# One list scheduler places every step of a scan, a router and eight experts

## The chip, the cores and the metric

The kernel runs on one core of a Trainium2 chip. Its time is the device time in microseconds (us) of one launch; the kernel before took 975.37 us, the median of three runs (975.14 to 976.99). Five engines work side by side, each through its own list of instructions in a fixed order: TensorE (PE in the rows), VectorE (DVE), ScalarE (ACT), GpSimd (POOL) and SyncE (SP), which here only issues transfers. They wait for each other by semaphores.

## The reference, cut to what matters

```python
sig = 1.0 / (1.0 + np.exp(-f_logit))
f = lower_bound + (1.0 - lower_bound) * sig          # x, f_logit: (4, 5056, 256)
for t in range(S):
    h = f[:, t] * h + (1.0 - f[:, t]) * x[:, t]
    y[:, t] = h
x = y.reshape(N, 256)                                 # N = 20224 tokens
logits = x @ w_gate                                   # 8 experts
e_idx = argmax(logits); gate_w = softmax(logits)[e_idx]
eom = 1.0 / (1.0 + np.exp(-(x @ w_output_gate)))
for e in range(8):
    m = e_idx == e
    out[m] = gate_w[m] * eom[m, e] * (np.maximum(x[m] @ w1[e], 0) @ w2[e])   # 256 -> 1024 -> 256
```

## The kernel before, in words

Tokens lie along the free axis and channels on the partitions. There are 40 chunks of 512 tokens, called c0 to c39 here; each goes through the same steps: loads (L257, L258), a tanh (L278), products (L282), the forget gates (L287), the scan (L293), a sum of squares (L300, L304) that sets a power of two as scale (L149 to L157, five short VectorE steps), the scaled values split in a high and a low fp16 part (L325 on ScalarE, L329 on VectorE), four DMA transposes that turn channels into rows (L320), the gate matmuls (L344), a short router on VectorE and ScalarE (L363 to L462) that ends with the row number of each token in its expert's list (`dst`, L448), and four row scatters on GpSimd (L467) into a scratch in DRAM, sorted by expert.

Each expert's two weight matrices, in two halves each, are loaded (L595), a Gram matmul gives a bound of their norm (L607, L614, L621), a power of two follows from it, and ScalarE and VectorE split them into high (L643) and low fp16 parts (L648). A product of two fp16 pairs is three matmuls.

Tiles of tokens of one expert are gathered from the scratch by a DMA transpose (`xq`, L660) that SyncE issues after it has read the tile's address. There are 16 early tiles of 128 tokens, two per expert in two rounds: the first round needs the rows of three chunks, the second of five. In an early tile each half of the up projection is 24 matmuls (L765 to L767), then a relu (L769, `eh`), its low part (L776, `el`), and each half of the down projection 12 matmuls (L785 to L787). 64 tiles of 256 follow (L712 to L714 up, L752 to L754 down), then smaller ones; their experts are chosen by a plan on VectorE, made whenever four more tiles are sure. The result is scaled (L679, L798) and scattered to the output (L802).

What sets the order: the first part, up to the first tile of 256, is written by loops over weight halves that pump a few stages of the chunks at a time, and a scheduler of the framework then moves instructions on some engines within it; from there on `experts` gives each quarter of a tile its share of the work by hand, in that order.

## Time and profile before

| what | value |
|---|---|
| median of three runs | 975.37 us |
| profiled execution, and its span in the trace | 981.98 us, 980.2 us |
| TensorE busy | 905.3 us (92% of the span) |
| VectorE, ScalarE, GpSimd busy | 796.2, 514.0, 382.1 us |
| mean granted clock of TensorE | 0.992 of 2.4 GHz |

Shares are means over stretches with different limits, so the rows further down are read by stretch. A line such as L712 is a line of the kernel before. A duration in a row is that of one instruction; neighbours on an engine overlap, so a distance between two starts is often shorter.

### The profile page before, as it was taken

The numbers are of one execution on the slowest core, as the hardware profiler recorded it, in microseconds if no ns is written. First come the engines' busy times: TensorE is split into PE (matmuls) and PEld (weight loads), VectorE is DVE, ScalarE is ACT, GpSimd is POOL, SyncE is SP. The second block draws the span as 40 slices with busy tenths as digits, with TensorE's granted clock in tenths as the row PEclk, the third lists the DMA queues.
The fourth block names the chain that finished last, engine by engine and source line by source line (L and its number), as shares of the span: only waits on it lengthen the run. The fifth ranks groups of instructions, "written<-read, shape, count | busy, mean of one in ns | idle before, by whom it ended". The sixth has DMA issues, their size and how long they took to land.

```text
span 980.2 us, 30989 instructions
## 1 busy us (share of the span) xinstructions
PE 905.3 (92%) x9775; PEld 813.9 (83%) x9775; DVE 796.2 (81%) x2683; ACT 514.0 (52%) x1075; POOL 382.1 (39%) x380
## 2 busy tenths in 40 slices
PE   2258878899999999999999999999999999999997
PEld 2247868788888888888888888888888888899986
DVE  7989877799898889888988889888898877846653
ACT  5667666555555555555555555555555543323332
POOL 1423324345444445543444454444444533312112
PEclk9999989999999999999999999999999999999999
DMA  8899973866555667565655555676665543412211
GB/s 312 208 286 290 247 211 95 184 149 146 151 157 155 153 140 153 143 148 145 167 153 149 138 154 139 147 165 155 145 154 138 151 118 84 118 44 50 50 35 34
DMA packets 236528, 146.16 MB, mean 149 GB/s; under 512 B 200508, under 2 KB 202173, under 8 KB 236369
## 3 DMA queue, kind: packets, MB, share of 16 engines
q1 hardware_dynamic: 220784, 101.34, 43.6%
q0 software_dynamic: 15296, 42.73, 14.5%
q8 instruction: 93, 1.52, 0.6%
q14 instruction: 67, 0.54, 0.2%
q10 hardware_dynamic: 288, 0.02, 0.0%
HBM read 58.38 MB, written 44.23 MB: 105 GB/s over the span
## 4 chain that ended last, share of the span: by engine, by line
PE 70%; issue 11%; DMA 9%; DVE 4%; POOL 3%; ACT 1%; SPq 1%; another core or an unknown queue 0%; POOLq 0%; DVEq 0%; ACTq 0%
PE ph L712 11%; PE py L752 11%; PE ph L714 11%; PE ph L713 10%; PE py L754 10%; PE py L753 10%; DMA xq<-scr 4%; DMA out_dram<-yo,mt 3%; POOL out_dram L802 2%; PE ph L765 1%; PE ph L767 1%; PE ph L766 1%; DMA w<-in_wT_dram 1%; PE pr L344 1%; PE pg L607 1%
## 5 line engine op out<-in xcount | busy, mean ns | idle before, releaser
L712 PE MATMUL ph<-xq,w 128*128 128x256 f16 (+2 forms) x1312 | 326.0, 259 | 1.0 <-DMA xq<-scr 1.0
L714 PE MATMUL ph<-xq,w 128*128 128x256 f16 (+2 forms) x1312 | 326.5, 259 | 0.2 <-issue 0.2
L713 PE MATMUL ph<-xq,w 128*128 128x256 f16 (+2 forms) x1312 | 326.3, 259 | 0.0
L717 ACT ACTIVATE hh<-ph 128x512 f16<-128x512 f32 (+1 forms) x312 | 173.4, 556 | 283.4 <-PE ph L714 246.3
L752 PE MATMUL py<-w2s,hh 128*128 x1136 | 309.0, 272 | 1.3 <-issue 0.7
L754 PE MATMUL py<-w2s,hl 128*128 x1136 | 309.4, 272 | 0.1
L753 PE MATMUL py<-w2s,hh 128*128 x1136 | 309.2, 272 | 0.0
L802 POOL DMA_INDIRECT out_dram<-yo,mt x146 | 153.6, 1052 | 308.7 <-ACT yo L798 255.5
L467 POOL DMA_INDIRECT scr<-rows,dst x154 | 191.9, 1246 | 182.9 <-issue 110.1
L725 DVE SCALAR_TENSOR_TENSOR hl<-ph,hh 128x512 f16<-128x512 f32 (+1 forms) x312 | 198.2, 635 | 44.5 <-ACT hh L717 28.3
L687 DVE COPY w<-w1s 128x2048 f16 x164 | 114.9, 701 | 44.7 <-PE ph L714 39.1
L712 PEld LDWEIGHTS <-w 128*128 128x128 f16 x1312 | 127.6, 97 | 12.7 <-DVE w L687 1.3
L714 PEld LDWEIGHTS <-w 128*128 128x128 f16 x1312 | 127.4, 97 | 11.9
L713 PEld LDWEIGHTS <-w 128*128 128x128 f16 x1312 | 127.3, 97 | 10.0 <-issue 0.3
L754 PEld LDWEIGHTS <-hl 128*128 128x128 f16 x1136 | 110.7, 97 | 13.8 <-issue 0.4
L752 PEld LDWEIGHTS <-hh 128*128 128x128 f16 x1136 | 110.8, 98 | 12.7 <-ACT hh L717 1.0
L753 PEld LDWEIGHTS <-hh 128*128 128x128 f16 x1136 | 110.7, 97 | 10.6
L293 DVE TENSOR_TENSOR_SCAN xt<-ft,xt 128x512 f32<-128x512 f32 (+4 forms) x78 | 90.8, 1172 | 0.0
L798 ACT ACTIVATE yo<-py,fac 128x256 f32<-128x256 f32 (+1 forms) x146 | 61.7, 467 | 26.9 <-PE py L754 25.7
L329 DVE SCALAR_TENSOR_TENSOR ft<-xt,sa,ft 128x512 f16<-128x512 f32 (+1 forms) x76 | 55.8, 739 | 20.6 <-ACT ft L278 19.9
L325 ACT ACTIVATE ft<-xt,sa 128x512 f16<-128x512 f32 (+1 forms) x76 | 50.2, 707 | 38.1 <-DVE li L312 29.1
L344 PEld LDWEIGHTS <-ft 128*128 128x128 f16 x600 | 51.3, 98 | 14.7 <-ACT ft L325 4.9
(189 smaller groups left out, 1353.4 us busy)
## 6 DMA issues: line engine op xcount, KB each, us to landing
ft<-in_fT_dram SPq DMA_DIRECT2D x37, 512.0 KB
xt<-in_xT_dram SPq DMA_DIRECT2D x37, 512.0 KB
w<-in_wT_dram SPq DMA_DIRECT2D x32, 512.0 KB
scr<-rows,dst POOLq DMA_INDIRECT x154
rows<-ft SPq DMA_TRANSPOSE x152
out_dram<-yo,mt POOLq DMA_INDIRECT x146
xq<-scr SPq DMA_TRANSPOSE x98
scr<-padt SPq DMA_DIRECT2D x9, 136.0 KB
```

The lines of the kernel that those rows point to most:

```text
L293: nc.vector.tensor_tensor_scan(out=xt[:, k, a:z], data0=ft[:, k, a:z], data1=xt[:, k, a:z], initial=init, op0=ALU.mult, op1=ALU.add)
L467: ins = nc.gpsimd.indirect_dma_start(out=scr[:, :], out_offset=IOA(ap=dst[:, b : b + 1], axis=0), in_=rows[:, b, :], in_offset=None)
L687: nc.vector.tensor_copy(out=w, in_=w1f[:, ds(T["ev"] * (2 * WH) + h * 2 * QH, 2 * QH)])
L712: nc.tensor.matmul(out=o, lhsT=w[:, f, k, 0, :], rhs=T["xh"][:, k, 0:n], start=first, stop=False)
L713: nc.tensor.matmul(out=o, lhsT=w[:, f, k, 0, :], rhs=T["xl"][:, k, 0:n], start=False, stop=False)
L714: nc.tensor.matmul(out=o, lhsT=w[:, f, k, 1, :], rhs=T["xh"][:, k, 0:n], start=False, stop=last)
L717: nc.scalar.activation(hh[:, :, 0:n], ph[:, :, 0:n], AF.Relu)
L725: nc.vector.scalar_tensor_tensor(out=hl[:, :, 0:n], in0=ph[:, :, 0:n], scalar=0.0, in1=hh[:, :, 0:n], op0=ALU.max, op1=ALU.subtract)
L752: nc.tensor.matmul(out=o, lhsT=hh[:, i, c], rhs=wh, start=first, stop=False, skip_group_check=True)
L753: nc.tensor.matmul(out=o, lhsT=hh[:, i, c], rhs=wl, start=False, stop=False, skip_group_check=True)
L754: nc.tensor.matmul(out=o, lhsT=hl[:, i, c], rhs=wh, start=False, stop=last, skip_group_check=True)
L802: ins = nc.gpsimd.indirect_dma_start(out=out[:, :], out_offset=IOA(ap=T["mt"][0 : T["p"], b, 2:4].bitcast(I32), axis=0), in_=T["yo"][0 : T ...
```

## The change

The loops and the pumping are gone. Every step is now an `Op` with an engine, a cost, the steps that it needs and a rank; `Clock.drive` simulates all engines at build time, takes at each point, among the steps that can start first, the one with the lowest rank, and emits the program in that order, which is then fixed on every engine. Ranks stand in a table by kind of step and chunk (shown in the diff by two lines).

With it come edits of the work itself. The first three chunks (FLIP) are turned into rows by 16 TensorE transposes each, and two ScalarE copies (`settle`), in place of four DMA transposes. Raw weights are loaded into the place of the next expert's fp16 weights, and all sixteen first loads follow each other. The norms of weights come in four groups (TEAMS), so that the five short scale steps run 4 times and not 16. For the first ten chunks (QUICK) eight more gate matmuls per chunk replace a ScalarE and a VectorE step. Small steps move from VectorE to ScalarE: the scales `sa` and `li`, the sum with 1 (`more_eg`), and the factors of early tiles. The early tiles follow a table of rounds and experts (ORDER). Where chunk 10 and later scatter rows, scatters stand at least 2.7 us apart in the simulated time (GAP), and all but a chunk's first are held behind the VectorE instruction that came last before them. A gather waits for those scatters only that no earlier gather has waited for.

```diff
+RANK = {
+    "setup": (-296.2,),
+    "pad": (-360.65,),
+    "steady": (147.22, -373.75, -143.82, 119.77, -79.5, -359.56, -45.81, 165.38,),
+    "tiles": (160.19, -324.31, -321.43, -288.45, -270.77, 131.32, -298.94,),
+    "first": (46.53,),
...
+FLIP = 3
+QUICK = 10
+NEAR = 0.2
+ORDER = ((0, 1), (0, 0), (0, 2), (1, 3), (1, 0), (0, 3), (1, 2), (0, 6), (0, 5), (1, 1), (1, 7), (0, 4), (1, 5), (1, 6), (0, 7), (1, 4))
+SHORT = 0.25
+TEAMS = ((0,), (1, 2), (3, 4), (5, 6, 7))
+GAP = 2.7
...
+    def start(self, o):
...
+        if o.gap:
+            t = max(t, self.sent + GAP)
...
+    def drive(self, lines, stop):
+        while not stop():
+            best = {}
+            lines = [line for line in lines if not line.over()]
+            for line in lines:
+                for o in line.heads():
+                    t = self.start(o)
+                    if t is not None:
+                        best.setdefault(o.eng, []).append((t, RANK[o.group[0]][o.group[1]] + o.shift, o))
+            assert best
+            pick = []
+            for e, c in best.items():
+                first = min(x[0] for x in c)
+                near = [x for x in c if x[0] <= first + NEAR]
+                p = min(near, key=lambda x: (x[1], x[0]))
+                fill = [x for x in near if x[2].cost <= SHORT and x[0] + 0.06 < p[0]]
+                pick.append(min(fill, key=lambda x: (x[1], x[0])) if fill else p)
+            t, _, o = min(pick, key=lambda x: x[0])
+            self.run(o, t)
+            for line in lines:
+                q = line.queues.get(o.eng)
+                if q and q[0] is o:
+                    q.pop(0)
...
-        nc.vector.tensor_scalar(sa, na, sx, None, ALU.mult)
-        nc.vector.tensor_tensor(out=li, in0=ix, in1=gi4, op=ALU.mult)
...
+            nc.scalar.activation(H["sa"], na, AF.Copy, scale=H["sx"])
...
+            nc.scalar.activation(H["li"], gi4, AF.Copy, scale=H["ix"])
...
+        def flip(i):
+            if i == 0:
+                H["rt"] = [pp.tile([P, 2, 2 * D], F16, tag="h", name="rt", bufs=4) for _ in range(nb // 2)]
+            for b in range(nb):
+                for k in range(KD):
+                    q = i * KD + k
+                    nc.tensor.transpose(
+                        out=H["rt"][b // 2][:, b % 2, q * P : (q + 1) * P], in_=hl[:, i, k, b * P : (b + 1) * P],
+                        identity=ident,
+                    )
+
+        def settle(j):
+            nc.scalar.activation(rows[:, 2 * j : 2 * j + 2, 0:CM].bitcast(F16), H["rt"][j], AF.Copy)
...
+                if i == 0 and quick:
+                    o, g = pr[:, b, 0:G], wgs[:, k, 1, :]
+                    nc.tensor.matmul(
+                        out=o, lhsT=hl[:, 0, k, tok], rhs=g, start=(k == 0), stop=False, skip_group_check=True
+                    )
...
+        def more_eg():
+            nc.scalar.activation(H["eg"][:, 0:nb], H["eg"][:, 0:nb], AF.Copy, bias=1.0)
...
+        if c < FLIP:
+            op(8, TEN, 0.5, lambda: flip(0), ["h0", "h1"], "flip", ring=("h", 4, (c, "settle1")), lazy=True)
+        turn1 = []
+        op(10, TEN, 0.45, all_gates, ["l0", "l1", ("setup", 11)], "pr", lag=2.8)
+        if c < FLIP:
+            op(10, TEN, 0.5, lambda: flip(1), ["l0", "l1"], ("turned", c), ring=("h", 4, (c, "settle1")), lazy=True)
+            for j in range(nb // 2):
+                op(10, ACT, 1.05, lambda j=j: settle(j), [("turned", c), *gone], f"settle{j}", lazy=True)
...
+            op(16, GPS, 1.32, lambda b=b: send(b), ["dst", "noted", "iota", *([f"settle{b // 2}"] if c < FLIP else ["turn00", "turn01", "turn10", ("turned", c)])],
+               "sent" if b == nb - 1 else None, ship=0.7, late=AHEAD <= c < NCH - 1 and b > 0, gap=AHEAD <= c < NCH - 1)
...
+    def crude(e, h, z):
+        if e == E - 1:
+            r = spare[:, h * WH : (h + 1) * WH]
+        else:
+            r = (w1f, w2f)[h][:, (e + 1) * 2 * WH : (e + 2) * 2 * WH].bitcast(F32)
+        return r[:, z * QH : (z + 1) * QH]
...
+        new = [k for k in new if id(k) not in waited]
...
-    ordered(0, prog["cut"])
+    ordered(0, 0)
```

SyncE, from where the last first loads of weights stand. Before, `ft` and `xt` are buffers of chunks, `w1s` and `w2s` places that c0 and c3 borrow:

```order
L595 DMA w_167<-in_wT_dram 128x1024
L595 DMA w_169<-in_wT_dram 128x1024
L320 DMA_TRANSPOSE w1s_126<-w2s_127 128x4x128 x4
L257 DMA w1s_126<-in_fT_dram 128x2x512
L258 DMA w1s_126<-in_xT_dram 128x2x512
L320 DMA_TRANSPOSE rows1_133<-ft_147 128x4x128 x4
L320 DMA_TRANSPOSE rows0_132<-ft_155 128x4x128 x4
L257 DMA ft_465<-in_fT_dram 128x2x512
L258 DMA xt_466<-in_xT_dram 128x2x512
L320 DMA_TRANSPOSE rows1_133<-w1s_126 128x4x128 x4
```

```order
L893 DMA w2s_119<-in_wT_dram 128x1024 x2
L893 DMA w1s_118<-in_wT_dram 128x1024 x2
L893 DMA w2s_119<-in_wT_dram 128x1024 x2
L445 DMA fx1_127<-in_fT_dram 128x2x512
L445 DMA fx1_127<-in_xT_dram 128x2x512
L445 DMA fx3_129<-in_fT_dram 128x2x512
L445 DMA fx3_129<-in_xT_dram 128x2x512
L893 DMA w1s_118<-in_wT_dram 128x1024
L893 DMA spare_125<-in_wT_dram 128x1024 x4
L893 DMA w1s_118<-in_wT_dram 128x1024
L893 DMA w2s_119<-in_wT_dram 128x1024
L994 TENSOR_LOAD pf_tab_705
```

Four transposes for each of c0, c1, c2 stood between the loads, and the next chunks' loads behind them; after, the loads of c3 and c4 (`fx1`, `fx3`) follow the weights and no transpose stands before the first gather's address is read.

ScalarE, around the first hi parts of weights (L643 before, L955 after). L363 are logit copies before; L525 and L529 are scales, L558 the copies of transposed rows after:

```order
L363 ACTIVATE lgp_283<-pr_258,li_227 128x128
L300 ACTIVATE ft_155,hss_212<-xt_156 128x512 x2
L417 ACTIVATE ex_357<-dl_306 128x32
L643 ACTIVATE w1s_126<-w_151,ws_299 128x8x128
L643 ACTIVATE w1s_126<-w_153,ws_299 128x8x128
L363 ACTIVATE lgp_362<-pr_330,li_256 128x128
L419 ACTIVATE eg_359<-gs_327 128x4
L325 ACTIVATE ft_155<-xt_156,sa_320 128x512 x2
L278 ACTIVATE w1s_126<-w1s_126 128x512 x2
L417 ACTIVATE ex_434<-dl_379 128x32
L363 ACTIVATE lgp_439<-pr_407,li_325 128x128
L287 ACTIVATE w1s_126<-w1s_126,fb_100,fa_99 128x512 x2
```

```order
L514 ACTIVATE fx0_126,hss_247<-fx0_126 128x512 x2
L529 ACTIVATE li_317<-gi4_113,xi_229 128x2
L955 ACTIVATE w1s_118<-w1s_118,ws_288 128x8x128
L529 ACTIVATE li_327<-gi4_113,xi_296 128x2
L955 ACTIVATE w1s_118<-w1s_118,ws_288 128x8x128
L525 ACTIVATE sa_339<-na_104,xs_295 128x2
L532 ACTIVATE fx3_129<-fx3_129,sa_339 128x512
L558 ACTIVATE spare_125<-rt_273 128x2x512
L558 ACTIVATE spare_125<-rt_274 128x2x512
L532 ACTIVATE fx3_129<-fx3_129,sa_339 128x512
L955 ACTIVATE w2s_119<-w2s_119,ws_288 128x4x256
L641 ACTIVATE ex_424<-dl_416,li_317 128x32
```

The first copies out of PSUM stand between the high parts (L532) of another chunk, with two more hi parts of weights behind them, and the logit copies are gone.

GpSimd, from the first scatter of rows (L467 before, L706 after) on; L802 and L1179 write an early tile's result:

```order
L467 DMA scr_72<-w1s_126,dst_381 162944x544 x4
L467 DMA scr_72<-rows1_133,dst_478 162944x544 x4
L467 DMA scr_72<-rows0_132,dst_537 162944x544 x4
L421 IOTA rows1_133 128x4
L421 IOTA rows0_132 128x4
L467 DMA scr_72<-rows1_133,dst_736 162944x544 x4
L421 IOTA rows1_133 128x4
L802 DMA out_0_dram<-ey_1001,mt_669 20224x256
L467 DMA scr_72<-rows0_132,dst_1141 162944x544 x4
L802 DMA out_0_dram<-ey_1244,mt_893 20224x256
```

```order
L706 DMA scr_75<-spare_125,dst_533 162944x544 x4
L706 DMA scr_75<-rows1_124,dst_568 162944x544 x2
L651 IOTA rows0_123 128x4
L706 DMA scr_75<-rows1_124,dst_568 162944x544 x2
L706 DMA scr_75<-rows0_123,dst_693 162944x544 x4
L1179 DMA out_0_dram<-ey_1074,mt_786 20224x256
L1179 DMA out_0_dram<-ey_1213,mt_830 20224x256
L651 IOTA rows0_123 128x4
L651 IOTA rows1_124 128x4
L706 DMA scr_75<-rows0_123,dst_1370 162944x544 x3
L706 DMA scr_75<-rows1_124,dst_1362 162944x544 x4
L651 IOTA rows1_124 128x4
```

c0 to c2 are scattered in one row in both. Before, c3's and c4's scatters stand one chunk at a time with a tile's result between them and the next; after, two results come first, and then c4's and c3's scatters nearly together.

## Rows read from the trace of the kernel before

**Rows 1.** Busy time by stretches: us, PE, PEld, DVE, ACT, POOL, granted clock, DMA, GB/s.

```profile
0.00:60.00 60.00, 14.48 (x179) 11.45 (x180) 49.59 (x191) 37.29 (x73) 15.80 (x35) 1.00 0.90 262
60.00:105.00 45.00, 36.78 (x504) 34.06 (x504) 41.08 (x139) 31.78 (x53) 15.10 (x14) 0.96 1.07 300
105.00:196.00 91.00, 78.52 (x1026) 70.77 (x1023) 69.37 (x241) 54.99 (x102) 32.59 (x32) 0.94 0.75 173
196.00:800.00 604.00, 603.35 (x6017) 540.67 (x6018) 529.50 (x1774) 328.73 (x700) 272.06 (x252) 1.00 0.60 149
```

**Rows 2.** The chain of waits, 40 to 200 us: start us, us, what.

```profile
43.79 2.08 ACT w2s L643 x2
...
54.80 5.81 DMA xq<-scr
...
80.05 4.77 DMA scr<-rows,dst
...
111.24 0.41 PE pr L344 x16
...
191.17 5.11 DMA xq<-scr
...
196.41 0.27 PE ph L712
```

**Rows 3.** The timeline of TensorE, 140 to 147 us: start us, us, engine, line.

```profile
143.29 0.22 PE L765 MATMUL ph<-xq,w1s 128*128 128x128 f16 x1
...
144.63 0.27 PE L785 MATMUL py<-w2s,eh 128*128 128x256 f16 x1
...
145.94 0.17 PE L621 MATMUL pb<-l,ones 128*128 128x1 bf16 x1
```

**Rows 4.** Groups by line and form, ScalarE, 0 to 188.8 us: busy us, mean ns.

```profile
L769 ACT ACTIVATE eh<-ph 128x512 f16<-128x512 f32 x32 | 18.8, 588 | 18.6 <-PE ph L767 9.4 <-remote 5.4 <-PE pb L621 2.6
L643 ACT ACTIVATE w1s<-w,ws 128x1024 f16<-128x1024 f32 x16 | 17.4, 1138 | 2.0 <-DVE ws L155 2.0
...
L798 ACT ACTIVATE ey<-py,fac 128x256 f32<-128x256 f32 x15 | 7.0, 465 | 10.4 <-PE py L787 5.0 <-remote 3.5 <-PE pr L344 1.9
L363 ACT ACTIVATE lgp<-pr,li 128x128 f32<-128x128 f32 x10 | 3.6, 362 | 12.6 <-remote 5.8 <-PE pr L344 5.0 <-PE ph L767 1.9
...
L417 ACT ACTIVATE ex<-dl 128x32 f32<-128x32 f32 x9 | 2.0, 221 | 1.7 <-DVE dl L383 1.0 <-issue 0.7
```

**Rows 5.** Groups of VectorE, 0 to 188.8 us, and its timeline at 75 us.

```profile
L329 DVE SCALAR_TENSOR_TENSOR ft<-xt,sa,ft 128x512 f16<-128x512 f32 x16 | 11.6, 742 | 0.0
...
L679 DVE TENSOR_SCALAR fac<-mt,cinv 128x1 f32<-128x1 f32 x16 | 3.3, 205 | 2.1 <-DMA mt<-scr 1.0 <-issue 1.0
...
L309 DVE TENSOR_SCALAR sa<-na,xs 128x2 f32<-128x2 f32 x10 | 2.5, 248 | 0.0
L149 DVE TENSOR_SCALAR wv<-pb 128x1 f32<-128x1 f32 x16 | 2.4, 148 | 0.3 <-PE pv L304 0.3
...
L368 DVE TENSOR_TENSOR lgo<-lgp 128x64 f32<-128x64 f32 x10 | 2.2, 216 | 5.1 <-ACT lgp L363 5.1
...
75.00 0.18 DVE L448 TENSOR_REDUCE dst<-pos 128x4 int32<-128x32 f32 x1
```

**Rows 6.** The timeline of GpSimd, 30 to 54 and 190 to 205 us.

```profile
33.96 1.46 POOL L467 DMA_INDIRECT scr<-w1s,dst  x1 [30.56 <-DVE w1s L282]
...
47.86 0.96 POOL L467 DMA_INDIRECT scr<-rows,dst  x1 [0.30 <-issue]
49.12 0.96 POOL L467 DMA_INDIRECT scr<-rows,dst  x1 [0.30 <-issue]
...
52.54 0.14 POOL L421 IOTA rows<- 128x4 int32 x1 [2.29 <-DMA scr<-rows,dst]
...
194.79 1.41 POOL L467 DMA_INDIRECT scr<-rows,dst  x1 [2.83 <-issue]
...
200.87 1.42 POOL L467 DMA_INDIRECT scr<-rows,dst  x1 [0.30 <-issue]
```

More of the change, by code (lines that the diff above doesn't have):

```diff
@@ L344, in gates @@
                 nc.tensor.matmul(
-                    out=o, lhsT=hl[:, i, k, tok], rhs=g, start=(i == 0 and k == 0), stop=(i == 1 and k == KD - 1),
+                    out=o, lhsT=hl[:, i, k, tok], rhs=g, start=(i == 0 and k == 0 and not quick), stop=(i == 1 and k == KD - 1),
                     skip_group_check=True,
                 )
-        for b in range(nb):
-            for i in range(2):
-                aside(gates, i, b)
-        when = LATER if between["on"] else (10, 10)
-        def turns(stage):
-            for k in range(KD):
-                if when[k] == stage:
-                    pace(turn(1, k))
@@ new lines, in chunk @@
+        for k in range(KD):
+            op(4, ACT, 0.75, lambda k=k: square(k), [f"scan{k}"] + ([(c - 2, "pv")] if c >= 2 else []), f"sq{k}")
+        op(5, TEN, 0.08, bound, ["sq0", "sq1", ("setup", 1), *past], "pv")
+        steps = pow2(H, lambda: pv, TX, "x", ("sx", "ix"))
+        chain(6, VEC, 0.19, steps[0], ["pv"])
+        for i, fn in enumerate(steps[1:4]):
+            chain(6, VEC, 0.18, fn, (), "sx" if i == 2 else None)
+        chain(6, VEC, 0.18, steps[4], (), "ix", lazy=True)
+        last.pop(VEC)
@@ new lines, in chunk @@
+        if not quick:
+            op(11, ACT, 0.34, logits, ["pr", "li"], "lgp")
+            chain(12, VEC, 0.22, sum_logits, ["lgp"], "lgo")
+        last[VEC] = "pr" if quick else "lgo"
+        for fn in (peak, below, keys, first_key, hot, own, gate):
+            chain(12, VEC, 0.21, fn, (), {below: "dl", hot: "oh", gate: "gs"}.get(fn))
+        if c >= AHEAD:
+            for x in turn1:
+                op(*x, ship=0.9, late=True)
+        op(14, TEN, 0.16, all_before, ["oh"], "pk", lag=1.4)
@@ L807, in put @@
             apart(ins, "out")
[L810 to L811 removed]
+    prog = {"places": ""}
     total = sure(N)
     unsure = (N - 256 * total - WHOLE * (P // 2 + 1) + E * (P - 1)) // P
[L814 to L829 removed]
@@ L977, in tile_scan_moe @@
-    while turns[-1] < E or line or pend or mid or over:
-        mine, rest = early(nh)
-        step(DRAIN, mine, LEAD)
-        rest()
-        if slots and prog["got"] == 0:
-            ahead(0)
-    prog["cut"] = len(nc.cur_bb.bb.instructions)
-    wp.release()
-    mpool["m"] = ctx.enter_context(tc.tile_pool(name="mp", bufs=2))
+    end = total + WHOLE + HALF
+    late = 2
+    last_put = end - late - REST
+    padded, known, tiles = {}, {}, {}
+    clock = Clock()
+    clock.tail = lambda: nc.cur_bb.bb.instructions[-1].name
@@ new lines, in tile_scan_moe, with spread, fn @@
+    clock.hold = lambda ins, name: tc.add_manual_dep(raw(ins), name, DATA, reason="pace")
+    clock.flush = beside
+    def spread(gen, count, needs, key, group, shift=0.0):
+        at = {}
+        def fn(i):
+            if i == 0:
+                at["g"] = gen()
+                next(at["g"])
+            kind = next(at["g"], None)
+            assert bool(kind) == (i < count - 1)
+        return [
+            Op(VEC, 0.2, lambda i=i: fn(i), needs if i == 0 else [(*key, i - 1)], key if i == count - 1 else (*key, i),
+               group=group, shift=shift)
+            for i in range(count)
+        ]
@@ new lines, in pad_op @@
+    def pad_op():
+        scattered["pad"] = [pad()]
+    lines = [Line(setup())]
+    for e in range(E):
+        lines.append(Line(expert_load(e)))
+        lines.append(Line(weights(e)))
+    chunks = []
+    for c in range(NCH):
+        lines.append(Line(chunk_load(c)))
+        chunks.append(chunk(c))
+        lines.append(Line([o for o in chunks[c] if not o.lazy and o.group[0] != "s"]))
+        lines.append(Line([o for o in chunks[c] if o.lazy]))
+    lines.append(Line([o for ops in chunks for o in ops if o.group[0] == "s"]))
@@ L987, in ordered @@
+    for t in range(end + 1):
+        for q in range(4):
+            work["pe"] += ([up(t, q)] if t < end else []) + ([down(t - 1, q)] if t else [])
+    lines += [Line(ops) for ops in work.values()]
+    clock.drive(lines, lambda: all(o.done for ops in work.values() for o in ops))
+    for line in lines:
+        assert line.over()
+    beside()
+    prog["got"] = end
     def ordered(start, cut):
@@ L995, in ordered, with experts @@
             prev[ins.engine] = ins.name
[L997 to L1000 removed]
+    def experts(t0, t1):
         for t in range(t0, t1 + 2):
+            if t < t1:
+                fetch(t)
             T = tiles.get(t) if t < t1 else None
```

1105 lines of the change are left out of this document (619 added, 486 removed), and 7 rows, old and new, of the table RANK.

## The prediction

> **What bounds the kernel now.** I read the busy time by stretches first, then the chain of waits, then single engines around the places that the chain names. The stretches [rows 1] say where anything can be won. From 196 to 800 us TensorE is busy 603.35 of 604 us at full clock. Before 196 us it is busy 14.48 + 36.78 + 78.52 = 129.8 of 196 us, so 66.2 us are idle there, and the granted clock of 105 to 196 us is 0.94. The diff keeps every matmul of the tiles, so a gain can come only out of these 196 us; after them an order can only lose.
>
> The chain of waits [rows 2] gives the events of the start. The gather of the first early tile is issued at 54.80 and takes 5.81 us, so TensorE begins early tiles at 60.6. The gathers of later tiles are what it waits for: behind the scatters of the fifth chunk (c4; chunks count from c0) rows land for 4.77 us from 80.05 to 84.8. The first tile of 256 has run alone when the gather of the next lands at 196.3 (191.17 + 5.11) and L712 starts at 196.41 for good. That lone first tile has 48 matmuls of L712 to L714 at 0.109 us (the spacing of the 256-column matmuls below), 5.2 us of work that is done, so before's steady stage behaves as one that began, without a gap, at 196.4 - 5.2 = 191.2. This is the mark that after has to beat.
>
> **The change part by part.**
>
> First chunks. The 12 DMA transposes of c0 to c2 leave SP; 48 transposes on TensorE and six copies on ScalarE take their place. TensorE is nearly empty there (14.48 of 60 us [rows 1]), so I take the spacing of its 128-column matmuls, 0.056 us ((144.63 - 143.29) / 24 [rows 3]): 48 x 0.056 = 2.7 us, beside other waits and at no cost. The upper bound is one matmul's whole duration each, 0.22: 10.6 us. A word of the Trainium skill on this, in two sentences that nothing else needs. "TensorE: Matmul & The Clock Gate", Part 4, gives about 275 ns for one 128x128 transpose inside a kernel, says that it needs a copy out of PSUM, and that such transposes don't hold the clock up; by it the 48 would be an estimated 13.2 us, and this speaks against the edit. No run here has such a transpose yet; the nearest row is the 0.22 us above.
>
> The copies (128x1024 f16 out of PSUM) have no row of their own either. The nearest are a ScalarE copy of that size out of SBUF, 1.138 us, and a relu of half the size out of PSUM, 0.588, twice 1.18 [rows 4]. I take 1.138, and as neighbours on ScalarE overlap by 0.10 (two copies of 1.138 in 2.08 us in the chain [rows 2]), 1.04 each.
>
> Where this lands: ScalarE stands in one queue from 7.5 us on, and the order shows what is before the place on which the fifth chunk rests (its L419 before, L646 after): 65 activations before, 88 after. By kind and with the overlap taken off: 6 copies x 1.04 = 6.2; 2 more hi parts of weights x 1.04 = 2.1; 4 more relus x 0.49 = 2.0 (three early tiles now stand ahead, one before); 2 evacuations x 0.365 = 0.7; 16 small ones that VectorE did (scales, +1, factors), 0.22 by L417 [rows 4], 0.12 with the overlap, = 1.9; minus 5 logit copies x 0.26 = 1.3. Sum 11.6 us. This is the term that costs. Its low end is 0, if the idle time of ScalarE hides it (31.78 of 45 us busy from 60 to 105 us [rows 1]).
>
> VectorE. Removed up to the first steady tile: 12 chains of five steps, 60 x 0.148 = 8.9; ten each of L309 and L368, 2.5 + 2.2, and the 16 factors, 3.3 [rows 5]; with three smaller kinds at 0.15 to 0.19 (23 of them, 3.9) some 21 us of durations. Up to c4's dst alone I get +2.0 us, as four more el and the rest of the Gram norms now come earlier and the short steps of a chunk follow each other directly, each waiting for the one before. VectorE is therefore not the later of the two engines at that place, ScalarE is.
>
> The fourth tile (T4). Before, c4's dst starts at 75.00 [rows 5]. After: 75.00 + 11.6 = 86.6. Both c3 and c4 are then scattered together: 8 scatters 1.26 apart (47.86 to 49.12 [rows 6]) are 10.1, so 96.7; the last lands 2.5 us after its end (50.08 to 52.54 [rows 6]; 4.77 at the worst [rows 2]), 99.2; and the gather takes 5.81 [rows 2]: 105.0. The three tiles ahead of T4 need no such time: their x comes some 3 us later than before, at 63.5 (the first scatter waits for some 6 us more of copies and small steps on ScalarE, about 40 instead of 33.96 [rows 6], and behind it the queue of twelve is the same, less the slow spacing of before's first ones), and three tiles are 3 x 2 x (1.34 + 1.31) = 15.9 us, over by 80. They fill idle time of TensorE; what T4 starts is then without a wait:
>
> From T4 to the first steady matmul. Half an up projection is 144.63 - 143.29 = 1.34 us, half a down 145.94 - 144.63 = 1.31 [rows 3]. Left are 26 x 1.34 + 28 x 1.31 = 71.5 us, and gates and counts of five chunks, about 0.8 each, 4.0 (24 gate matmuls at 0.026, by the 16 in 0.41 us of the chain [rows 2], are 0.6): 75.5. The clock costs too: 0.94 on average from 105 to 196 us [rows 1], between full speed and the lower level, is some 5.5 us, in a stretch that has idle times; with fewer of them I take 3.0. First steady matmul 105.0 + 75.5 + 3.0 = 183.5. By their orders and the rows' means VectorE and ScalarE have 64 and 61 us of work in these 78 us and don't bound it, and by the same count the dst of the eighth chunk, the last that the first steady tiles need, comes near 138.
>
> Steady stage. Scatters are held at least 2.7 us apart: four take 8.1 us instead of 200.87 - 194.79 = 6.1 [rows 6]. Price 0 as long as a plan's rows are waited for by a gather that TensorE reaches later; at worst 2 us for each plan of four tiles, 16 of them, 32 us. I take 0, as TensorE has no idle there now [rows 1]. The moves from VectorE to ScalarE in it are 0 as well: neither bounds.
>
> Sum. 183.5 - 191.2 = -7.7 us on the profiled execution of 981.98 (span 980.2 and 1.8 around it): 974.3. It stands 6.6 us above the median of the runs, 975.37, so 967.7 there.
>
> **The rivals.**
>
> More is won. ScalarE's 20 us of idle before c4 take up the 11.6, and only VectorE's +2.0 delays c4: dst 77.0, T4 95.4, first steady matmul 173.9, a gain of 17.3: 958.1. For it: ScalarE is busy 37.29 of the first 60 us and 31.78 of the next 45 [rows 1]; the SP queue is free of 12 transposes. Against: each chunk's chain crosses both engines in turn, so that idle is waiting and not room.
>
> The other side: the copies block ScalarE's queue. Each pair stands ahead of ready work and waits until TensorE has transposed and VectorE has made the low part. If the 16 transposes of a chunk take 0.22 each one after another, 3.5 us, and the two low parts ahead of them 2 x 0.74 = 1.5 more [rows 5], a pair costs 5.0 us of wait, three pairs 15.1. T4 goes to 120.1, the first steady matmul to 198.6, 7.4 later than the mark: 982.8. It decides from T4 = 112.7, that is 7.7 us of waits. For it: in the order the first pair stands between the two high parts of another chunk, with three hi parts of weights behind it. Against: hi parts of weights and scales stand between a chunk's high parts and its copies, and give the other engines time.
>
> Nothing that can be told. T4's delay and the 66 us of idle balance: T4 between 110.7 and 114.7, time 973.4 to 977.4. For it: before already overlaps the early tiles with the preparation, and 66 us of idle can be moved and not taken out. Or the steady stage gives back what the start gains.
>
> The change costs in the steady stage. Every instruction's place is now fixed on its engine, and a scatter that waits out its 2.7 us holds the writes of tiles behind it on GpSimd. One wait of 1 us of TensorE per plan is 16 us: 967.7 + 16 = 983.7. Against: gathers are placed tiles ahead, and GpSimd has time (272.06 of 604 us busy [rows 1]).
>
> **How the numbers follow.** Chances: the forecast 0.40 (964 to 972, by one us or two of ScalarE's sum and of the clock), more is won 0.24, nothing 0.13, blocked copies 0.16, steady stage 0.07. Two tenths of a per cent, about 2 us, is what a measurement of this kernel can tell from no change. Faster takes the first two: 0.64; same 0.13; slower 0.23. For the range I take 952, below the second by 6 for a still earlier T4, and at the top 983, the two slower cases; a tenth is left out on each side.
>
> **What would show it.** In the profile after: c4's dst near 87 and later than before; the fourth early tile's first matmul near 105, TensorE without idle from there to a first steady matmul near 183; the copies at about 1.1 us; the last 780 us like before's. I am wrong if early tiles still wait for gathers past 105, if the copies stand in ScalarE's queue idle, if the first steady tile again waits for the second's rows, or if TensorE shows idle past 200.

## The result, and the profile after

The changed kernel took 988.64 us (median of four runs, 987.38 to 991.23), the kernel before 976.18 beside it (975.14 to 978.04): a ratio of 1.0129, with an interval of 1.0102 to 1.0156. It is 12.5 us slower, where 8 us faster was forecast. The profiled execution took 987.38 us, its span 985.3.

Busy time by stretches, after, columns as in [rows 1]:

```profile
0.00:60.00 60.00, 25.82 (x298) 22.00 (x298) 45.17 (x149) 42.75 (x75) 17.14 (x35) 0.80 0.88 299
60.00:105.00 45.00, 28.59 (x389) 25.63 (x389) 30.07 (x109) 21.42 (x49) 9.04 (x10) 0.77 0.93 233
105.00:196.00 91.00, 76.10 (x1073) 71.26 (x1074) 79.95 (x203) 71.31 (x144) 39.35 (x37) 0.91 0.71 154
196.00:800.00 604.00, 603.68 (x6037) 541.16 (x6036) 483.18 (x1430) 354.30 (x788) 241.72 (x255) 1.00 0.65 150
```

From 196 us on nothing is lost here: TensorE is busy 603.68 of 604 us. The loss lies ahead. From 60 to 105 us TensorE is busy 8.2 us less than before and at the granted clock 0.77 instead of 0.96, between 1.2 and 2.4 GHz, and VectorE and ScalarE are less busy too. Everything waits. The timeline of TensorE, after, has the three marks: the first matmul of the first early tile, of the fourth, and of the steady stage.

```profile
66.31 0.27 PE L1116 MATMUL ph<-xq,w1s 128*128 128x128 f16 x1 [1.25 <-DMA xq<-scr]
...
116.84 0.27 PE L1116 MATMUL ph<-xq,w1s 128*128 128x128 f16 x1 [13.34 <-DMA xq<-scr]
...
197.84 0.27 PE L1050 MATMUL ph<-xq,w 128*128 128x256 f16 x1
```

The steady stage begins at 197.84, 6.6 us behind the mark of 191.2; what follows it is as long as before (985.3 - 197.84 = 787.5 against 980.2 - 191.2 = 789.0). So the profiles differ by 5.4 us and the runs by 12.5: before's one profiled execution was 5.8 us above the median of its own four runs, after's 1.3 below.

What the fourth tile waits for is on VectorE, after, from 60 us on; the brackets hold the idle time before a row and what ended it. It answers [rows 5], where c4's dst stands at 75.00:

```profile
71.97 0.29 DVE L938 SCALAR_TENSOR_TENSOR jk<-pg,ident 128x128 f16<-128x128 f32 x1 [4.93 <-PE pg L932]
...
77.99 1.29 DVE L496 SCALAR_TENSOR_TENSOR fx<-fx 128x512 f32<-128x512 f32 x2 [1.27 <-DMA fx<-in_xT_dram]
...
90.12 0.19 DVE L599 TENSOR_REDUCE mx<-rw 128x4 f32<-128x32 f32 x1 [0.90 <-PE rw L572]
...
94.85 0.18 DVE L681 TENSOR_REDUCE dst<-pos 128x4 int32<-128x32 f32 x1
95.25 0.19 DVE L681 TENSOR_REDUCE dst<-pos 128x4 int32<-128x32 f32 x1
```

The Gram step of expert 6's weights (L938) waits 4.93 us for TensorE, where the Gram stands behind half of the first early tile and then waits for weights that SyncE loads behind the first gather. Behind it on VectorE, in the fixed order, stand that tile's low parts, then c4's products (L496), then the routers of c3 and c4. The scatters follow, on GpSimd, after:

```profile
97.58 1.00 POOL L706 DMA_INDIRECT scr<-rows,dst  x1 [6.09 <-DVE xi L313]
...
109.02 0.13 POOL L651 IOTA rows<- 128x4 int32 x1 [1.62 <-DMA scr<-rows,dst]
109.70 1.58 POOL L706 DMA_INDIRECT scr<-rows,dst  x1 [0.55 <-issue]
```

Last, what SyncE waited for from 30 to 112 us, after (total us, times, longest). L542 are the transposes of a chunk, L893 loads weights, L445 chunks:

```profile
SPq L542 <- DMA scr<-rows,dst: 8.9, 2, 7.7
SPq L893 <- DVE jk L938: 8.6, 3, 6.1
SPq L893 <- DVE fx L506: 4.6, 3, 1.9
SPq L893 <- DVE w1s L959: 3.9, 1, 3.9
SPq L445 <- DVE fx L535: 2.5, 1, 2.5
...
SPq L445 <- DVE fc L698: 2.2, 1, 2.2
```

The rows of L893 and L445 that end with VectorE are together 38.7 us of these 82: the code holds every load behind the VectorE instruction placed last ahead of it (`elif (o.bulk or o.late) and self.last: self.hold(made, self.last)` in `Clock.run`). In the kernel before the loads of weights (L595) wait 8.7 us for VectorE in the same stretch, its largest row being

```profile
SPq L595 <- DVE w1s L648: 4.4, 3, 3.0
```

and the loads of chunks none. A wait of this kind does not occur in the sum of the prediction. Nor does that of the first row: three transposes of c5 wait until c3's rows, in whose buffer they write, have landed, and in the order of SyncE they stand ahead of the gather of the fourth tile (L998):

```profile
109.01 3.84 SPq L542 DMA_TRANSPOSE rows<-fx  x3
...
113.99 1.22 SPq L998 DMA_TRANSPOSE xq<-scr  x1
```

### The profile page after: what moved, and what is told of

Its sections match the earlier page's. It is cut to its first block, busy times and chain, and to the rows that moved or that the text cites. A ratio compares the mean times of both kernels' runs of the same rounds, so it can differ in the third digit from the quotient of the medians.

```text
span 985.3 us, 30656 instructions
## 1 busy us (share of the span) xinstructions
PE 912.0 (93%) x9891; PEld 822.7 (83%) x9891; DVE 749.2 (76%) x2207; ACT 553.8 (56%) x1207; POOL 353.2 (36%) x381
## 4 chain that ended last, share of the span: by engine, by line
PE 70%; DMA 10%; issue 7%; DVE 7%; POOL 2%; ACT 1%; SPq 1%; POOLq 0%; DVEq 0%; ACTq 0%
PE ph L1050 11%; PE py L1094 11%; PE ph L1052 11%; PE ph L1051 11%; PE py L1096 11%; PE py L1095 11%; DMA out_dram<-yo,mt 3%; DMA fx<-in_xT_dram 3%; DVE fx L506 2%; DMA w1s<-in_wT_dram 2%; POOL out_dram L1179 1%; PE rw L572 1%; DVE w2s L959 1%; DMA fx<-in_fT_dram 1%; DVE fx L496 1%
## 5 line engine op out<-in xcount | busy, mean ns | idle before, releaser
L1179 POOL DMA_INDIRECT out_dram<-yo,mt x146 | 153.1, 1049 | 287.6 <-ACT yo L1175 239.4
L706 POOL DMA_INDIRECT scr<-rows,dst x154 | 165.1, 1072 | 239.6 <-DVE fx L535 48.0
L506 DVE TENSOR_TENSOR_SCAN fx<-fx,fx 128x512 f32<-128x512 f32 (+4 forms) x78 | 96.4, 1241 | 5.9 <-ACT fx L501 5.9
L501 ACT ACTIVATE fx<-fx,fb,fa 128x512 f32<-128x512 f32 (+1 forms) x80 | 62.3, 802 | 39.0 <-DVE fx L496 38.6
L535 DVE SCALAR_TENSOR_TENSOR fx<-fx,sa 128x512 f16<-128x512 f32 (+1 forms) x80 | 55.9, 739 | 15.2 <-ACT fx L532 15.2
L496 DVE SCALAR_TENSOR_TENSOR fx<-fx 128x512 f32<-128x512 f32 (+1 forms) x80 | 52.3, 678 | 19.1 <-DMA fx<-in_xT_dram 19.0
```

Of the source, the lines that this page charges most:

```text
L506: nc.vector.tensor_tensor_scan(out=xt[:, k, a:z], data0=ft[:, k, a:z], data1=xt[:, k, a:z], initial=init, op0=ALU.mult, op1=ALU.add)
L706: ins = nc.gpsimd.indirect_dma_start(out=scr[:, :], out_offset=IOA(ap=H["dst"][:, b : b + 1], axis=0), in_=rows[:, b, :], in_offset=None)
L1179: ins = nc.gpsimd.indirect_dma_start(out=out[:, :], out_offset=IOA(ap=T["mt"][0 : T["p"], b, 2:4].bitcast(I32), axis=0), in_=T["yo"][0 : T ...
```

## The experiments

Chips differ, so each ratio is to the kernel before on the same chip. Letters of theories hold within the runs that were started together.

### The same kernels on other chips

The kernel before, and the changed kernel three times, without an edit:

> The kernel before, unchanged, for a second profile. Its first profiled execution took 981.98 us against a median of 976.18 of its timed runs. Theory 1 (that execution was a late one): this profile is near 976 and its first lasting L712 begins some 6 us before 196.41, so that the distance to the changed kernel in the start is near 12 us. Rival (profiling costs this kernel 6 us): the profile is again near 982 and L712 begins at 196 to 197.

> The changed kernel, unchanged, on the chip of these runs. In the last runs three kernels that differ from it by a few instructions in the first 110 us took 1027 us, and TensorE ran 4 per cent fewer matmuls from 400 to 800 us than in the changed kernel's first profile, with granted clock 1.0; the kernel before took 984 there, not 976. Theory C (the loss lies with the chip or its memory, which the changed kernel's order of the steady stage tolerates less than before's): where before takes about 984, this kernel takes about 1025; where before takes about 976, it takes 988, and TensorE has no idle from 400 to 800 us. Rival D (the moves of those kernels themselves cost it): this kernel takes 988 to 998 whatever before takes.

> The changed kernel once more, as the mark on this chip for the three runs beside it. On two of the three chips seen so far it took 1027 to 1033 us and on one 988; either is possible here. Its first matmul of the fourth early tile should come at 116 to 117 us, its first steady matmul between 198 and 209 us.

> The changed kernel as the mark on this chip: 985 to 992 us or 1024 to 1034, its fourth early tile's first matmul at 116 to 117 us and its first steady matmul between 198 and 209 us.

Before against itself: 986.01 us, 1.000 (0.9975 to 1.0025). Its profiled execution took 987.45 us, so profiling does not by itself cost 6 us; but the chip was another one, and where the first profile of the kernel before lost its 5.8 us stays open. The changed kernel in three runs on two further chips: 1032.79 (1.0455, 1.0400 to 1.0509), 1026.22 (1.0414, 1.0353 to 1.0474), 1030.57 (1.0469, 1.0385 to 1.0552). So the first chip was the mild one, as theory C had it: elsewhere the same program costs 42 to 46 us. Its start is alike up to the fourth tile (116.15, 115.9 and 115.6). From there on TensorE pauses: from 117 to 200 us it is idle for 5 to 6 us in which the trace shows it waiting for nothing, where the first chip has no such time; the steady stage begins at 208.6, 202.93 and 204.63 for 197.84, and what follows takes 32 to 33 us longer. Stretch 400 to 800, of the first such run:

```profile
400.00:800.00 400.00, 389.93 (x3801) 340.47 (x3799) 301.96 (x898) 225.26 (x498) 151.56 (x160) 1.00 0.61 143
```

### Single steps of the start

Loads of c4 and the last quarter of expert 6's weights ahead of the first gather; four DMA transposes per chunk again, in place of transposes on TensorE and the copies; one GpSimd step that waited, behind c4's last scatter:

```diff
+MOVES = ((("f", 4), ("first", 0, "x")), (("x", 4), ("first", 0, "x")), (("w", 6, 1, 1), ("first", 0, "x")))
```
```diff
-                    nc.tensor.transpose(
...
+            for k in range(KD):
+                turn(i, k)
...
-            nc.scalar.activation(rows[:, 2 * j : 2 * j + 2, 0:CM].bitcast(F16), H["rt"][j], AF.Copy)
+            pass
```
```diff
+MOVES = (((4, "sent"), (5, "iota")),)
```

> The changed kernel with three transfers moved on SP alone: both loads of c4 and the last quarter of expert 6's weights stand ahead of the first gather instead of among the first three gathers; every other engine's order is the same, word for word. Theory A (c4's dst is late because its load is queued behind gathers that wait for scatters): c4's products, at 77.99 us in the changed kernel, start by 73, c4's dst moves from 95.25 to 91 or less and the time falls by 3 to 5 us to about 984. Rival B (the steps of c4 stand in the queues of ScalarE and VectorE behind those of three early tiles, whatever the load does): c4's products start at 75 to 77 and the time changes by less than 2 us.

> The changed kernel with one part undone: c0 to c2 are turned by four DMA transposes each, issued on SP at the places where the TensorE transposes stood, and the six ScalarE copies are gone; all else stands in the same order. Rival from the prediction (the copies and transposes block ScalarE and TensorE): the time falls by 5 us or more, to 983 or less, and c0's dst comes before 37. Theory A (SP's queue is what the start waits for): 12 transposes, some 16 us of SP's time, push the weights and c3's loads back, the first early tile starts at 72 or later instead of 66.31, and the time rises by 5 to 15 us.

> The changed kernel with one instruction moved on GpSimd alone: c4's last scatter stands ahead of the iota of c5, which in the changed kernel waits 1.62 us for c3's rows to land and holds that scatter. If the scatters of c3 and c4 are on the path to the fourth early tile, that tile starts 1.5 to 2 us earlier than 116.84 and the time falls by as much, to about 986.8. If the fourth tile waits for its expert's weights instead (their last low parts of the up projection end at 110.4), it starts at the same time within 0.5 us and the time stays within 1 us.

1027.39 (1.0418), 1030.31 (1.0468) and 1027.28 (1.0429), intervals of 0.004 to 0.007 either way, where the changed kernel has 1.0414 to 1.0469 on such chips: none changes the time by more than can be told. The changed kernel itself was not run on this chip, and the times near 985 us that were expected belong to the first one. The loads ahead were the miss that taught most. c4's products began at 79.96 and its dst came at 98.6, not earlier, and VectorE's wait for the Gram only grew. The loads then stood right ahead of the first gather; from its issue to the first matmul it took 7.0 us, for 2.9 to 4.2 in the changed kernel:

```profile
75.86 0.29 DVE L955 SCALAR_TENSOR_TENSOR jk<-pg,ident 128x128 f16<-128x128 f32 x1 [7.04 <-PE pg L949]
```

With DMA transposes the first early tile came at 73.0, as theory A had it, c0's dst at 38.5, and the last scatter of c0 to c2 began at 64.5 instead of 56 to 60, so undoing the copies gives the start nothing. Without the step in their way the eight scatters began within 9.1 us instead of 12.1, and the gather still left at 116.28, 6.6 us after the end of the last of them, behind the three transposes of c5 on SyncE.

### Late holds taken away

```diff
-        elif (o.bulk or o.late) and self.last:
+        elif o.bulk and self.last:
```

> The changed kernel without the holds of the steady stage: scatters of rows and the second two transposes of a chunk no longer wait for the VectorE instruction ahead of them in the program, and are issued as soon as their data and queue allow; the order on every engine is the same. If the holds keep transfers out of each other's way, transfers bunch again, the mean scatter takes longer than 1.07 us (before: 1.25) and the time rises by up to 10 us; if the steady stage hides all of it (TensorE 603.68 of 604 us busy), the time is within 2 us of the changed kernel's beside it.

1075.82, 1.0871 (1.0805 to 1.0938), beside 1.0455: the holds of late scatters and transposes, which I had priced as a possible cost, save 43 us on that chip. That is four times what was expected at most, and not by the way that was expected: between 200 and 900 us the mean scatter took 1.03 us, not longer than 1.07.

### Row transfers that come three at a time

Counting in the traces, between 200 and 900 us, what a pause of TensorE (over 0.25 us, not waiting for data) follows gave one thing: a row transfer of GpSimd (scatter or result) that starts less than 2.9 us after the start of the last but one. One case, GpSimd and then TensorE, in the first of those runs:

```profile
412.37 1.22 POOL L706 DMA_INDIRECT scr<-rows,dst  x1 [2.02 <-DVE fx L535]
413.89 1.00 POOL L1179 DMA_INDIRECT out_dram<-yo,mt  x1 [0.30 <-issue]
415.19 1.07 POOL L1179 DMA_INDIRECT out_dram<-yo,mt  x1 [0.31 <-issue]
```
```profile
416.16 0.21 PE L572 MATMUL rw<-wgs,fx 128*128 128x32 f16 x2
416.92 0.27 PE L1050 MATMUL ph<-xq,w 128*128 128x256 f16 x1 [0.55 <-issue]
```

The weight load of the same matmul pauses as well, and waits for nothing that the trace shows ("issue"):

```profile
416.90 0.10 PEld L1050 LDWEIGHTS <-w 128*128 128x128 f16 x1 [0.62 <-issue]
```

The edit lets the emitted order stand and holds such a third back, behind the VectorE instruction that comes last before 3.5 us (4.3 in the second run) after the last but one in planned time:

```diff
+                for i, f in enumerate(o.rows):
+                    t = max(o.at + 1.3 * i, free)
+                    at = max(t, sent[-2] + BURST) if len(sent) > 1 else t
...
+            made = f()
+            if (o.late or slow) and self.last:
+                self.hold(made, self.last)
```

> Same work and same order; in the steady stage a row transfer on GpSimd (a scatter of rows or a write of a tile's result) that would be the third within 3.5 us in the planned time is held behind the VectorE instruction that comes last before that point, 56 of 236 of them. Theory D (TensorE pauses when a third row transfer starts within about 3.2 us of two others: on the chips where the changed kernel took 1030 us, 26 to 29 of the 52 to 57 such thirds between 200 and 900 us were followed by a pause of 0.3 to 1.3 us on TensorE, and only 0 to 2 of 190 others): the pauses between 200 and 900 us fall from some 35 to fewer than 10, and the time is 15 to 35 us below the changed kernel on this chip if that takes some 1030, and within 3 us of it if that takes some 988. Rival E (the pauses come from TensorE's own queue, or from the rows being late): the pauses stay above 25 and the time stays within 5 us of the changed kernel.

> The changed kernel's order; thirds of row transfers held within 4.3 us of planned time instead of 3.5. With 3.5 the thirds that came within 3.2 us on the chip fell from 57 to 21, the pauses of TensorE from 41 to 15 and the time by 18 us. Theory D: thirds below 15, pauses below 10 and the time 20 to 30 us below the changed kernel where that takes some 1030. Rival: the holds now delay what waits for rows or for buffers of results, the pauses fall but the time stays where it was with 3.5 or rises.

1008.3 us, 1.0227 (1.0165 to 1.0289), beside 1026.22; and 1009.37, 1.0194 (1.0119 to 1.0268), beside 1030.57: 18 and 21 us less. TensorE from 400 to 800 us in the first of them:

```profile
400.00:800.00 400.00, 396.69 (x3922) 351.93 (x3921) 313.60 (x936) 232.47 (x516) 164.27 (x166) 1.00 0.66 149
```

| kernel | such thirds | with a pause | all pauses, waits included, us |
|---|---|---|---|
| before, first chip / another | 6 / 6 | 2 / 4 | 1.7 / 2.8 |
| changed, first chip | 53 | 0 | 0.4 |
| changed, others | 50 to 54 | 29 to 34 | 25.7 to 27.2 |
| late holds taken away | 79 | 37 | 53.6 |
| thirds held 3.5 / 4.3 us | 19 / 8 | 10 / 4 | 9.7 / 10.1 |

Fewer thirds, fewer pauses and less time, in both directions. Of the 53.6 us without the late holds 23 are waits for other engines or for rows, so not all of that loss is of this kind. By count, waits included, the pauses fell from 41 to 15 and from 39 to 13, not below 10 as expected of both; six of the last 13 are waits.

### c3 and c4 ahead of the early tiles

Two orders were written by hand, of some two dozen moves each. These are the core of the second; the first lacked the last line's first entry, had the Gram of expert 6 ahead of the gates, and left c5's steps and the loads of expert 5's weights in their places:

```diff
+    ([("f", 4), ("x", 4)], ("w", 6, 0, 0)),
+    ([(4, "m0"), (4, "m1")], ("lo", 1, 0, 0)),
+    ([(4, "scan0"), (4, "scan1")], ("lo", 1, 1, 0)),
+    ([(c, k) for c in (3, 4) for k in ("l0", "l1")], ("lo", 2, 0, 1)),
...
+    ([(3, "pr"), (4, "pr"), (4, "pk"), (3, "pk"), ("gram", 4, 0), ("gram", 4, 1), ("pb", 2), ("gram", 6, 1)], ("first", 0, "up", 0)),
+    ([("first", 0, "put"), ("first", 1, "put")], ("first", 2, "put")),
```

> Same work and same waits; only the order on the engines is changed between some 40 and 100 us, so that the fourth and fifth chunk (c3, c4) with their router, and the weights of experts 3 and 4, stand ahead of the first three early tiles on VectorE, ScalarE, TensorE and SyncE, where the changed kernel has them behind. Theory A (c4's rows are late because its chain stands behind the first early tiles, which wait for a gather, on in-order engines): c4's dst from 95 us to 72 to 80, the fourth tile's first matmul from 117 to 95 to 102, the first steady matmul 12 to 18 us earlier than in the changed kernel on this chip, and the time too. Rival B (the transfers bound this part, since the DMA engines are 0.93 busy from 60 to 105 us): the loads only change places, dst comes before 90 but scatters and the gather take the gain back; the fourth tile at 112 or later and the time within 4 us of the changed kernel. Rival C (the weights of expert 3 are next): dst near 75, but the fourth tile waits for them until 108 or later.

> The order of the run with c3 and c4 ahead of the first early tiles, and the thirds of the row transfers held, in one kernel. If theories A and D hold, their gains add: 12 to 18 us at the start and, on a chip where the changed kernel takes some 1030 us, 15 to 35 in the steady stage, which would bring the kernel to 965 to 985 us, level with or below the kernel before. If only one holds, the time is that of the one run that is faster.

> The order with c3 and c4 ahead of the first early tiles again, without the two blocks that the run before showed: there c4's dst came at 84 instead of 95 us, but TensorE's gate matmuls stood 7 us behind a Gram of weights that were loaded behind the first gather, and GpSimd's scatters 13 us behind the write of the first tile. Now that Gram stands behind the gates, the writes of the first two tiles behind the scatters, and the transposes of c3 ahead of the first gather. Theory A (the order costs at the start what it lost against the kernel before): c4's dst 72 to 80, the first of its scatters by 84, the fourth early tile 96 to 103 instead of 116, and the time 10 to 20 us below the changed kernel on this chip. Rival F (the start is bound by the sum of the work, so whatever goes ahead puts something else behind, as in the run before, where c5 came 8 us later): dst early again, but the first steady matmul within 5 us of the changed kernel's, and the time too.

> That order and, in the steady stage, row transfers held so that no third is planned within 4.3 us. If theories A and D hold: below the changed kernel by the sum of the two single runs beside it; on a chip where the changed kernel takes some 1030 us that is 985 to 1000, on one where it takes some 988 it is 970 to 980, below the kernel before.

All four missed: 1033.7 (1.0479, 1.0412 to 1.0546) and 1035.24 (1.0485, 1.0424 to 1.0547) with the order alone, 1016.41 (1.0334) and 1013.82 (1.0260) with thirds held. c4's dst did come at 84.2 and 79.7, yet the fourth tile began at 117.6 and 118.3. Each time another wait took the place. In the first order GpSimd's scatters stood behind the first tile's result:

```profile
98.64 1.20 POOL L1276 DMA_INDIRECT out_dram<-ey,mt  x1 [37.22 <-ACT ey L1272]
99.81 0.30 POOL L745 IOTA rows<- 128x4 int32 x2
100.29 1.98 POOL L800 DMA_INDIRECT scr<-rows,dst  x1 [0.18 <-DVE fx L600]
```

In the second SyncE stood 12.8 us at the load of c6, held behind a VectorE step, with the gather behind it (waits of SyncE, 90 to 125 us):

```profile
SPq L543 <- DVE cinv L1049: 12.8, 1, 12.8
```

### Early loads not held

```diff
-        elif (o.bulk or o.late) and self.last:
+        elif (o.bulk and self.on or o.late) and self.last:
```

> Same order and work; before the first steady tile the loads of chunks and weights are no longer held behind the VectorE instruction that was placed last before each of them (the changed kernel holds every one; 34 of the first 60 SyncE instructions that wait, wait for VectorE, here 6). If these holds cost the start, the loads of the weights of experts 5 and 4, issued from 80 to 95 us, come within some 5 us of each other, expert 3's weights are ready by 98 instead of 113, c6's load leaves near 88 instead of 97, and the time is 3 to 8 us below the changed kernel (1024 to 1034 on the slower chips, 988 on the first). If the order alone decides, c4's dst stays at 94 to 98, the fourth early tile at 115 to 118, and the time within 3 us of it.

> The order with c3 and c4 ahead of the first early tiles, and the early loads not held. In the run with that order alone the rows' numbers came at 79 us and the last scatter ended at 100, but SyncE stood from 97 to 109.5 at the load of c6, which was held behind a VectorE step of the weights, with the gather of the fourth tile behind it. Theory A with that hold gone: the gather at 103 or before, the fourth early tile at 102 to 108 instead of 118, the first steady matmul 8 to 14 us earlier than in that run (211.0), 197 to 203, and the time 8 to 14 us below it. Rival F: another wait takes its place, the fourth tile after 112, the time as it was.

> The same with row transfers held so that no third is planned within 4.3 us in the steady stage. The sum of the two: 20 us below the run without these holds on a chip of the slower kind, so 995 to 1005; on a chip of the first kind 975 to 985.

> The changed kernel's order, early loads not held, thirds of row transfers held within 4.3 us. On a chip of the slower kind 18 to 22 us below the run with free loads alone, so 1000 to 1010; on a chip of the first kind equal to it.

On a chip of the slower kind, before at 984.97: 1018.11 (1.0331, 1.0286 to 1.0375) with the changed kernel's order, 1013.8 (1.0300, 1.0259 to 1.0341) with the second order, 992.95 (1.0079, 1.0049 to 1.0108) with that and thirds held, 998.96 (1.0149, 1.0093 to 1.0204) with the changed order and thirds held. The changed kernel was not run on this chip, so the gain of free loads is read between ratios: 0.8 to 1.4 per cent with its order and thirds as they are, 0.5 to 0.8 with thirds held (within 4.3 and 3.5 us beside it; intervals overlap), and 1.8 to 1.9 with the order by hand. With the changed kernel's order c4's dst came at 89.2 and 93.95 and the fourth tile at 109.44 and 112.95, so the holds did cost the start. In the run with the second order and free loads alone c4's dst, the fourth tile and the steady stage:

```profile
72.99 0.19 DVE L780 TENSOR_REDUCE dst<-pos 128x4 int32<-128x32 f32 x1
```
```profile
102.72 0.27 PE L1218 MATMUL ph<-xq,w1s 128*128 128x128 f16 x1
...
192.07 0.27 PE L1152 MATMUL ph<-xq,w 128*128 128x256 f16 x1
```

The dst is 22 us earlier than in the changed kernel and 2 earlier than before; the tile comes where I had forecast it for the changed kernel (105.0). The steady stage begins at 192.07, 11 to 17 us ahead of the changed kernel on such chips and level with the kernel before on one of them (191.72), but 89.4 us after the fourth tile, not 78.5. None of these kernels is as fast as the one before; the best is 8 us behind.

## Why the prediction was wrong, point by point

**The step that failed is c4's dst.** I took before's 75.00 and added 11.6 us, the durations of what ScalarE does more ahead of that place; VectorE, "+2.0", was "not the later of the two". It came at 95.25. ScalarE's sum was about right: up to that place it is busy 59.60 us for 47.24 before. But it was not the price. VectorE is busy 68.84 us for 62.34, 6.5 more where I had 2.0, and the other 13.8 of the 20.3 us are idle time of VectorE: in a fixed order an instruction also pays for what those ahead of it wait for, L938 for a Gram behind an early tile, the low parts for that tile, L496 for a load. The runs show it from both sides. Brought ahead of the early tiles the same chain gives 79.7, and 72.99 when the loads are free as well, with ScalarE busy 53.70 us up to it, still 6.5 more than before. These runs were on chips of the slower kind; on the first one no edit of the changed kernel was run. The busy times up to c4's dst, columns as in [rows 1], before, after, and in the run with the second order and free loads:

```profile
0.00:75.00 75.00, 26.68 (x342) 23.13 (x343) 62.34 (x242) 47.24 (x90) 22.07 (x41) 1.00 0.94 272
0.00:95.25 95.25, 51.42 (x641) 45.05 (x641) 68.84 (x223) 59.60 (x112) 20.29 (x39) 0.80 0.90 268
0.00:72.99 72.99, 30.26 (x396) 26.90 (x397) 58.33 (x197) 53.70 (x98) 16.02 (x37) 0.73 0.97 350
```

**A wait that the sum lacks.** Every early load is held behind VectorE. Taking the holds away gave 4 to 14 us with the changed order and 18 with the other one, by ratios. The order by hand gains only once they are gone, and little: 0.3 per cent with thirds as they are, 0.7 with thirds held (both times the intervals overlap, the second time barely).

**A reading.** Of the four chunk loads behind the first weights I called those into `fx3` c4's; they are c5's. c4's two loads stand among the first three gathers, at 69.30 and 73.45. Moving them alone changed nothing, so it is not the cause.

**The rest of the fourth tile's delay.** It came at 116.84 for 105.0: 8.65 us from dst; 2.3 from dst to the first scatter, which I took as nothing; 3.6 from the scatters (111.28 - 97.58 = 13.7 for 10.1: three long ones and the step that waited 1.62); 0.2 from the landing to the gather; the gather 3 shorter than 5.81. The landing alone did not set the gather: SyncE came to it from the three transposes of c5, which ended at 112.85, about when the last rows landed, and the run with the scatters closer together shows that these transposes hold it back even when the rows are there.

**Half of the 12.5 us.** The mark of 191.2 was read from an execution that took 6.6 us more than the median, and the sum was then taken off the median. If that excess lies ahead of the steady stage, the mark was as much too late; no run shows where it lies.

**Right.** The first scatter at 39.05 (about 40); the copies at 1.01 us each, of which one waited, 1.30 us for TensorE, so the rival of blocked copies falls. That its fourth tile (120.1) and first steady matmul (198.6) come close to 116.84 and 197.84 is chance, as its wait is not there. From the fourth tile to the steady stage it took 81.0 us for 78.5, and the steady stage of that chip lost nothing.

**The steady stage elsewhere.** I named waits for rows as the danger and gave it 0.07. In the three runs on other chips rows were waited for 0.2 us at most. On the other chips TensorE pauses behind bursts of row transfers, of which the change makes 53 where before had 6, since results and scatters now follow each other in 1.30 us. Holding thirds gave back 17 to 21 us in six pairs of runs, nearly half of what these chips lose; free loads and the order by hand gave 11 to 15 more (1.0194 and 1.0227 to 1.0079).

**Open.** Why the first chip shows 53 bursts and no pause with the changed kernel, and what in the chip pauses TensorE. Transfers of instructions, which the traces hold too, are no likely cause: from 1 us before a pause to its end one was under way in 26 of 69 pauses of two runs, as many as their share of the time would give. Open is also what the last 8 us are; some 5 lie ahead of the steady stage, which begins at 197.07 in that run and at 191.72 in the kernel before on another such chip. The kernel with both edits was not run on a chip of the first kind.

## What to carry to other kernels

When a planner fixes the order on engines that work in order, price a moved step by what the instructions ahead of it wait for, engine by engine, SyncE and GpSimd included; the durations on VectorE were 6.5 of 20.3 us here. List every wait that a change adds, those for pacing too: a hold that helps in a full stage (43 us here) can cost in a start that is waiting. On chips like the slower ones here, keep row transfers of GpSimd from coming three within 3 us, and time a tuned order on more than one chip.

## What the runs showed of the hardware

The pauses are the surprise: 0.3 to 1.3 us in which TensorE waits for nothing that the trace shows and issues no matmul, in 29 to 34 of the 50 to 54 cases in which a third row transfer starts within 2.9 us, on some chips and not on another, with the same program. Quite free of them the first chip is not: the kernel before has 2 there, after 2 of its 6 thirds. At spacings over 2.9 us they are rare (41 thirds at 2.9 to 3.2 us in either profile of the kernel before: none). The Trainium skill ("DMA: Bandwidth & Descriptors", on latency and other measured facts) says that transfers issued by GpSimd keep their descriptors in rings in SBUF, and its guess, called not certain there, is that contention at the ports of these rings makes two of the DMA engines slower; no run here shows whether TensorE's reads meet them.

Sixteen transposes on TensorE took 1.87 us, 0.117 us each in a row, at the lower of the two clock levels (granted clock 0.50 from 46 to 48 us). Sixteen matmuls of the same shape took as long at that level, and 1.19 us between 35 and 38 us, where the granted clock is 0.91:

```profile
36.33 1.19 PE L932 MATMUL pg<-w1s 128*128 128x128 bf16 x16
...
46.04 1.87 PE L552 MATMUL rt<-ident,fx 128*128 128x128 f16 x16
...
48.91 1.87 PE L932 MATMUL pg<-w2s 128*128 128x128 bf16 x16
```

So the prediction's 0.056 us, read at full clock, was half of what a transpose took, 5.6 us for the 48 instead of 2.7. By the Trainium skill's 275 ns for one ("TensorE: Matmul & The Clock Gate", Part 4) sixteen would be an estimated 4.4 us. The measurement decides: one alone lasts 314 ns here, near that figure, but in a row the next one starts after less than half of it.
